# Fetches of stored weights go from SyncE's queue to GpSimd's, and the first gated phase's weights are narrowed one expert earlier

## The chip, the cores and the metric

The kernel runs on one core of a Trainium2 chip. Its time is the device time of one launch in microseconds: 1245.48 us as the median of three runs (1244.81 to 1248.36). Five engines work side by side, each with a queue of its own that it works off in the order in which it is written: TensorE (PE; its weight loads PEld), VectorE (DVE), ScalarE (ACT), GpSimd (POOL) and SyncE (SP), which here only begins DMA transfers. ScalarE and GpSimd can begin transfers too. All transfers share 16 DMA engines.

## What is computed

Three layers follow one another. Attention over 4 x 12 heads of 448 positions gives 1792 tokens of 768 values. A router sends each token to one of 8 experts; an expert is `relu(x @ w1[e]) @ w2[e]` with 1024 hidden values, times the router's probability. A gated layer ends it:

```python
x = attn_out.transpose(0, 2, 1, 3).reshape(1792, 768)
for e in range(8):
    h = np.maximum(x[mask_e] @ w1[e], 0.0)
    out[mask_e] = gate_w[mask_e, None] * (h @ w2[e])
gate = 1.0 / (1.0 + np.exp(-(out @ w_gate)))     # 768 x 1536, stored as float64
val = out @ w_val                                # 768 x 1536, stored as float64
return (gate * val @ w_out)                      # 1536 x 768, stored as float64
```

w_gate, w_val and w_out come as float64, in DRAM as pairs of 32-bit integers. The kernel itself puts each of them together as float32, which the text calls narrowing.

## The kernel before

**The stages.** Attention and the routing fill the first 378 us. The experts follow one by one (378 to 735), sorted by the number of their tokens, so that expert e works on a window of fixed size: 320, 288, 264, 248, 240, 236, 224 and 224 tokens. Then come twelve phases of the gated layer (735 to 1061; gate and value by turns, 128 columns of each half at a time, in seven products of block sums instead of eight), and the projection by w_out (1061 to 1226).

**One expert.** Everything stands under a manual schedule: each engine does what is written for it in the order of the code. The first layer has eight chunks f. Each is 18 matmuls (`hidden`: six blocks of the contraction, three products of high and low parts, by `product`, L987), then `relu`: ScalarE writes the high part of the hidden values (hhl, L1036) and VectorE the low part (L1037). The second layer has six chunks o of 24 matmuls. Each begins with two or three transposes of the next expert's window (`window_turn`, L1025; the parts xhl at L981 and L982) and ends with a copy xo on ScalarE (L1095) and a store of it, begun by ScalarE (L1096), into the array of all tokens, x2. The second layer needs all eight chunks of the first.

**The expert weights.** An expert has seven pieces, four of w1 (768 KB) and three of w2 (1 MB). SyncE loads them into three buffers "raw" (`piece_load`, L820). Behind every chunk `advance` splits half of the piece that is two ahead: ScalarE the high part (whl, L831), VectorE the low part (L835). Every second chunk it begins the load of the piece three ahead.

**What is woven in.** In experts 2 to 6, behind each of the 14 chunks, `out_narrow` takes a step: either it begins the fetch of a 128 x 384 block of w_out into one of two buffers raw64 (`out_fetch`, L1253, on SyncE), or it narrows one: four VectorE operations (L1222, L1225, L1231, L1234), an addition on GpSimd (L1237) and a store of the block to DRAM, begun by GpSimd (L1269). There are 24 blocks. `early_sums` has GpSimd form parts of the gated layer's input sums in experts 5 and 6 (L1307) and store them into x2 (L1310). In expert 7 `glu_weights` does for four blocks of w_gate, the first phase's weights B11, B12, B22 and B21, what was done for w_out (fetched on SyncE, L1348; kept on the chip), forms their sums T3, T2, T1 and T4 (L1374) and splits them (`w_split`). `glu_ahead` does three blocks of the second phase in expert 7's second layer. Narrowed blocks and early sums take turns in six buffers v. `window_load(e + 1)` (L1014 and L1016, on SyncE) fetches the next expert's tokens at the start of an expert.

**The first gated phase.** `glu` holds a table of jobs by slot (slot i stands behind the i-th of the phase's 14 groups of matmuls, counted from 0; -1 ahead of the phase): casts and differences of input blocks (`both`, `parts`, L1274 and L1277), sums of blocks (`sums`, L1307; `fourth`, L1474). Evictions of the products are L1541 and L1546.

Of the kernel before, what the change touches and what calls it, by code (L numbers as in the profile page):

```python
# [21 lines left out]
def tile_attention_moe_glu(  # L22
# [966 lines left out]
    def experts(pools):  # L989
# [55 lines left out]
        for e in range(E):  # L1045
            n = WIN[e]
            hh = ho.tile([128, 2, nfc, CAP], F32R, tag="hhl", name="hhl")[:, :, :, 0:n]
            if 0 < e < E - 1:
                window_load(e + 1)
# [11 lines left out]
            if e == 0:  # L1061
                window_load(1)
            for f in range(nfc):
                if f < ahead:
                    ps = pss4[f]
                else:
                    ps = gemm_ps()[:, :n]
                    for c in range(NC):
                        hidden(e, f, ps, c)
# [178 lines left out]
    def out_fetch(pools):  # L1248
        if out_at[0] < len(outs):
# [3 lines left out]
            nc.sync.dma_start(out=out_raw[-1][2], in_=wo64[f * 128 : (f + 1) * 128, h * ND : (h + 1) * ND])  # L1253

    def out_narrow(pools):
# [5 lines left out]
        if step < 2 or (out_at[2] and step * len(outs) // 68 == (step - 1) * len(outs) // 68):  # L1261
            out_fetch(pools) if len(out_raw) < 2 else None
        elif out_raw:
# [5 lines left out]
            nc.gpsimd.dma_start(out=wod[f][:, h * ND : (h + 1) * ND], in_=v)  # L1269

# [69 lines left out]
    fetched = {}  # L1340

    def fetch(pools, i):
        if i < len(fetches):
# [4 lines left out]
            nc.sync.dma_start(out=t, in_=w64[k % 2][:, r * HC : (r + 1) * HC, m * 128 : (m + 1) * 128])  # L1348
# [48 lines left out]

    def glu_weights(pools, f, xw):

        if f == 0:  # L1400
            ws.extend([xw[:, i].rearrange("p (a c t) -> p a c t", a=2, c=HC)[:, a] for a in range(2)] for i in range(3))
            for i in range(2):
                fetch(pools, i)
        elif f < 5:
            for step in range(2):
                v_narrow(pools, 0, V_FIRST[f - 1], step)
            if f == 2:
                w_split(pools, 0, 1)
            elif f == 3:
                v_sum(pools, 0, "T3")  # L1410
                v_sum(pools, 0, "T2")
        elif f == 5:
            w_split(pools, 0, 7)
        elif f == 6:
            w_split(pools, 0, 6)
            v_sum(pools, 0, "T1")
        elif f == 7:
            v_sum(pools, 0, "T4")
# [21 lines left out]
    def glu(pools):  # L1440
        pools["wq"].release()
# [47 lines left out]
        for slot, f, *a in (  # L1489
            (-1, both, 1, "A11"), (-1, both, 0, "S1"), (-1, sums, "S1", s1, nc.gpsimd), (-1, sums, "S2", s2, nc.gpsimd),  # L1490
            (1, both, 0, "A12"), (1, w_split, pools, 0, 5), (2, w_split, pools, 0, 2), (2, fourth),
            (3, both, 1, "A12"), (3, parts, 0, "S4", s4), (4, parts, 1, "S1", s1), (5, both, 1, "A22"),
# [270 lines left out]
```

## Time and profile before

| | |
|---|---|
| median of three runs | 1245.48 us |
| the profiled execution, its span | 1246.61 us, 1244.9 us |
| TensorE busy | 1151.9 us, 93% |
| VectorE, ScalarE, GpSimd busy | 844.6, 620.4, 532.7 us |

The profile is of one execution. In the rows below, a row of the table of stretches has the window in us, its length, the busy time of TensorE, of its weight loads, of VectorE, ScalarE and GpSimd (each with its count of instructions), the granted clock of TensorE as a share of full speed, the mean busy share of the DMA engines and GB/s. A timeline row has the start, the duration, the engine, the line, the operation, what it writes and reads, and in brackets how long the engine stood idle before it and what ended that. A row of waits says which line waited for what: us in total, times, longest. In the chain of waits each piece follows from the one above it, to the end of the program.

### The profile page before, as it was taken

What the parts mean: (1) busy time and instruction counts of PE and PEld (TensorE: products, weight loads), DVE (VectorE), ACT (ScalarE), POOL (GpSimd) and SP (SyncE); (2) the same over time, 40 slices, a digit from 0 to 9 for tenths busy, and PEclk for the clock granted to TensorE, in tenths of its full rate; (3) what the DMA queues carried; (4) which work ended last, traced back from release to release, by engine and by line L of the source; (5) the groups of instructions that cost most, each with busy time, mean ns of one, the idle gap of its engine ahead of it and who ended that gap; (6) DMA issues with size and microseconds to landing.
All of it is one profiled execution on the core that took longest, in us unless ns stands there. A gap on an engine that the chain in (4) does not pass through costs nothing.

```text
span 1244.9 us, 20296 instructions
## 1 busy us (share of the span) xinstructions
PE 1151.9 (93%) x7312; PEld 1061.2 (85%) x7313; DVE 844.6 (68%) x1424; ACT 620.4 (50%) x1363; POOL 532.7 (43%) x654
## 2 busy tenths in 40 slices
PE   4999999999968999988988887999999999999997
PEld 3778888887957999987888886999999999999997
DVE  7999898897874556678677879768776774422110
ACT  5788998998963444444434445333332324321110
POOL 5656779777430001212334253747566464011110
PEclk9999999999988999989989977999999999999999
DMA  5315613121027567777879620323223234532220
GB/s 131 92 31 161 198 46 89 48 56 33 1 80 237 161 200 243 249 248 241 262 237 304 208 90 13 104 73 130 81 96 111 76 110 150 189 127 77 89 76 38
DMA packets 125323, 161.50 MB, mean 130 GB/s; under 512 B 6495, under 2 KB 111327, under 8 KB 125219
## 3 DMA queue, kind: packets, MB, share of 16 engines
q1 hardware_dynamic: 113331, 135.86, 35.5%
q0 software_dynamic: 4704, 17.80, 4.0%
q10 hardware_dynamic: 7184, 6.50, 1.6%
q8 instruction: 59, 0.97, 0.3%
q14 instruction: 45, 0.37, 0.1%
HBM read 117.19 MB, written 34.60 MB: 122 GB/s over the span
## 4 chain that ended last, share of the span: by engine, by line
PE 50%; DVE 7%; DMA 7%; issue 2%; ACT 2%; ACTq 0%; POOL 0%; SPq 0%; POOLq 0%; DVEq 0%
PE psg L1519 24%; PE pso L987 13%; PE psg L987 12%; DMA raw<-in_moe_w_dram 5%; DVE whl L835 2%; DMA x<-xo 1%; ACT whl L831 1%; DVE v L1225 1%; PE psw L1025 1%; DMA raw<-in_moe_w_gate_dram 1%; DVE sx L1277 1%; DVE e L1234 1%; DVE x L1277 1%; PE psw L850 1%; DVE hhl L1037 1%
## 5 line engine op out<-in xcount | busy, mean ns | idle before, releaser
L1237 POOL TENSOR_TENSOR v<-v,e 128x384 f32<-128x384 f32 x72 | 74.6, 1036 | 329.3 <-DVE e L1234 318.9
L835 DVE TENSOR_TENSOR whl<-raw,whl 128x768 fp32r<-128x768 f32 (+1 forms) x112 | 137.8, 1231 | 88.3 <-ACT whl L831 85.6
L987 PE MATMUL psg<-hhl,whl 128*128 128x224 f32 (+6 forms) x1152 | 167.1, 304 | 20.9 <-DVE hhl L1037 13.1
L987 PEld LDWEIGHTS psg<-hhl,whl 128*128 128x128 f32 x1152 | 156.2, 207 | 24.3 <-DVE hhl L1037 12.0
L987 PE MATMUL psg<-xhl,whl 128*128 128x224 f32 (+6 forms) x1152 | 145.6, 285 | 8.1 <-DVE whl L835 4.8
L987 PEld LDWEIGHTS psg<-xhl,whl 128*128 128x128 f32 x1152 | 140.2, 189 | 11.9 <-DVE whl L835 6.4
L831 ACT CAST whl<-raw 128x768 fp32r<-128x768 f32 (+1 forms) x112 | 103.2, 923 | 84.2 <-DMA raw<-in_moe_w_dram 51.7
L333 ACT ACTIVATE pn<-pss,nm 112x448 f32<-112x448 f32 x184 | 119.9, 652 | 26.1 <-DVE nm L322 24.4
L322 DVE TENSOR_REDUCE nm<-pss 112x1 f32<-112x448 f32 x192 | 118.3, 616 | 11.3 <-PE pss L315 10.9
L987 PE MATMUL pso<-sx,x 128*128 128x384 f32 x720 | 125.0, 334 | 0.0
L987 PEld LDWEIGHTS pso<-sx,x 128*128 128x128 f32 x720 | 124.8, 188 | 0.0
L370 DVE TENSOR_TENSOR pl<-pst,ph 112x448 fp32r<-112x448 f32 x180 | 110.5, 614 | 18.3 <-ACT ph L357 16.9
L1519 PE MATMUL psg<-sx,xw 128*128 128x448 f32 x420 | 112.0, 375 | 2.9 <-ACT sx L1274 2.9
L350 PEld LDWEIGHTS pst<-ident,pn 112*112 112x112 f32 x768 | 88.6, 135 | 26.7 <-DVE pl L370 6.8
L350 PE MATMUL pst<-ident,pn 112*112 112x112 f32 x768 | 107.0, 262 | 4.6 <-DVE pl L370 4.3
L357 ACT CAST ph<-pst 112x448 fp32r<-112x448 f32 x180 | 97.5, 542 | 9.8 <-PE pst L350 7.0
L384 PE MATMUL psv<-ph,vt 112*128 112x448 f32 x204 | 92.1, 461 | 0.0
L315 PE MATMUL pss<-kh,qt 128*112 128x448 f32 x192 | 79.5, 414 | 12.1 <-ACT pn L333 11.0
L1519 PEld LDWEIGHTS psg<-sx,xw 128*128 128x128 f32 x420 | 81.1, 193 | 11.1 <-ACT sx L1274 3.9
L714 POOL DMA_INDIRECT out_dram<-sg,idx x14 | 17.4, 1242 | 160.0 <-DVE sg L1652 98.1
L1519 PE MATMUL psg<-sx,x 128*128 128x448 f32 x297 | 75.8, 366 | 0.9 <-DVE sx L1277 0.9
L315 PE MATMUL pss<-kl,qt 128*112 128x448 f32 x192 | 72.1, 376 | 0.0
(275 smaller groups left out, 2394.2 us busy)
## 6 DMA issues: line engine op xcount, KB each, us to landing
raw<-in_moe_w_dram SPq DMA_DIRECT2D x32, 768.0 KB, 7.1
raw<-in_moe_w_dram SPq DMA_DIRECT2D x24, 1024.0 KB, 7.7
hd<-sg SPq DMA_DIRECT2D x48, 224.0 KB, 1.9
raw<-in_moe_w_out_dram SPq DMA_DIRECT2D x24, 384.0 KB, 5.0
raw<-in_moe_w_gate_dram SPq DMA_DIRECT2D x24, 384.0 KB, 3.3
raw<-in_moe_w_val_dram SPq DMA_DIRECT2D x24, 384.0 KB, 3.4
xs<-zero SPq DMA_DIRECT2D x8, 960.0 KB, 8.1
x<-hd SPq DMA_DIRECT2D x5, 1536.0 KB, 7.6
```

The lines of the kernel that those rows point to most:

```text
L315: nc.tensor.matmul(ps[:P, :S], lhsT=qt[:, r * P : (r + 1) * P], rhs=kk, start=(i == 0), stop=(i == 1))
L322: nc.vector.tensor_reduce(out=nm, in_=sc[n, r][:P, :S], axis=AX.X, op=ALU.max, negate=True)
L333: nc.scalar.activation(out=pn[n][:, r], in_=sc.pop((n, r))[:P, :S], func=AF.Exp, bias=sc.pop((n, r, "m")), scale=scale(0, 0, n, 1)[:, r] i ...
L350: nc.tensor.transpose(ps[:P, r * P : (r + 1) * P], p[:, r, c * P : (c + 1) * P], ident[:P, :P])
L357: nc.scalar.copy(out=ph, in_=pt[n, c][0][:P, :S])
L370: nc.vector.tensor_tensor(out=pl, in0=ps[:P, :S], in1=ph.bitcast(F32), op=ALU.subtract)
L384: nc.tensor.matmul(ps[:, :S], lhsT=lhs, rhs=p, start=(c == 0 and i == 0), stop=(c == R - 1 and i == len(parts) - 1),)
L831: nc.scalar.copy(out=splits[p][:, 0, cs], in_=raws[p][:, cs])
L835: nc.vector.tensor_tensor(out=w[:, 1, cs], in0=raws[p][:, cs], in1=w.bitcast(F32)[:, 0, cs], op=ALU.subtract)
L987: nc.tensor.matmul(ps, lhsT=lhs[:, a], rhs=rhs[:, b], start=first and i == 0, stop=last and i == 2)
L1237: nc.gpsimd.tensor_tensor(out=v, in0=v, in1=e, op=ALU.add)
L1519: nc.tensor.matmul(ps, lhsT=w[a][:, c], rhs=x[b][:, c], start=(n == 0 and j in (1, 2, 7)), stop=(n == 3 * HC - 1), skip_group_check=j not ...
```

## The change

The fetches of w_out and, until the gated layer starts, of w_gate and w_val are begun by GpSimd, right behind the addition and the store of a narrowed block. The steps at which blocks are narrowed are spread by another formula (57 steps for the 24 blocks), which gives 4, 6, 6, 6 and 2 of them in experts 2 to 6. The four w_gate blocks of the first phase are narrowed at steps 61, 63, 65 and 67, which is in expert 6 (its chunks f5, f7, o1 and o3), and T3 and T2 are formed at o4 and o5; expert 7 keeps T1, T4 and the splits, at earlier chunks. The window load of the next expert stands at an expert's fourth chunk. In the first gated phase four jobs stand in later slots, so that evictions come ahead of casts.

```diff
--- before.py
+++ after.py
@@ -1045,8 +1045,6 @@
         for e in range(E):
             n = WIN[e]
             hh = ho.tile([128, 2, nfc, CAP], F32R, tag="hhl", name="hhl")[:, :, :, 0:n]
-            if 0 < e < E - 1:
-                window_load(e + 1)
             roff = nc.scalar.value_load(table_i[0:1, 2, e : e + 1], min_val=0, max_val=NT if e else 0)
             ahead = 2 if e == 0 else 0
             pss4 = [gemm_ps()[:, :n] for f in range(ahead)]
@@ -1058,9 +1056,9 @@
                 if c:
                     for f in range(ahead):
                         hidden(e, f, pss4[f], c - 1)
-            if e == 0:
-                window_load(1)
             for f in range(nfc):
+                if f == 3 and e + 1 < E:
+                    window_load(e + 1)
                 if f < ahead:
                     ps = pss4[f]
                 else:
@@ -1250,7 +1248,9 @@
             f, h = outs[out_at[0]]
             out_at[0] += 1
             out_raw.append((f, h, raw_tile(pools)))
-            nc.sync.dma_start(out=out_raw[-1][2], in_=wo64[f * 128 : (f + 1) * 128, h * ND : (h + 1) * ND])
+            nc.gpsimd.dma_start(out=out_raw[-1][2], in_=wo64[f * 128 : (f + 1) * 128, h * ND : (h + 1) * ND])
+
+    OUT_STEPS = 57
 
     def out_narrow(pools):
 
@@ -1258,15 +1258,22 @@
         out_at[1] += 1
         if step == 0:
             st_open(pools)
-        if step < 2 or (out_at[2] and step * len(outs) // 68 == (step - 1) * len(outs) // 68):
-            out_fetch(pools) if len(out_raw) < 2 else None
-        elif out_raw:
+            for _ in range(2):
+                out_fetch(pools)
+        n = len(outs)
+        if step > 2 and (step - 2) * n // OUT_STEPS > (step - 3) * n // OUT_STEPS and out_raw:
             f, h, raw = out_raw.pop(0)
             v = vs[out_at[2] % len(vs)]
             out_at[2] += 1
             narrow_a(raw, v)
             narrow_b(raw, v, es[0])
             nc.gpsimd.dma_start(out=wod[f][:, h * ND : (h + 1) * ND], in_=v)
+            if out_at[0] < n:
+                out_fetch(pools)
+            else:
+                fetch(pools, len(fetched))
+        elif step in V_STEPS:
+            glu_first(pools, V_STEPS.index(step))
 
 
 
@@ -1338,6 +1345,8 @@
     V_OF = {1: "B11", 2: "B21", 6: "T2", 7: "T3", 5: "B12", 4: "B21", 3: "B22"}
     fetches = [(k, n) for k in range(PHASES) for n in (V_NAMES if k else V_FIRST)]
     fetched = {}
+    glu_queue = [nc.gpsimd]
+    V_STEPS = (61, 63, 65, 67, 68, 69)
 
     def fetch(pools, i):
         if i < len(fetches):
@@ -1345,7 +1354,7 @@
             r, c = int(n[1]) - 1, int(n[2]) - 1
             m = k // 2 + c * HM
             t = fetched[i] = raw_tile(pools)
-            nc.sync.dma_start(out=t, in_=w64[k % 2][:, r * HC : (r + 1) * HC, m * 128 : (m + 1) * 128])
+            glu_queue[0].dma_start(out=t, in_=w64[k % 2][:, r * HC : (r + 1) * HC, m * 128 : (m + 1) * 128])
 
     V_SLOT = {"B11": 4, "B21": 5, "B12": 0, "B22": 3, "T3": 1, "T2": 2}
     V_SLOT0 = {"B11": 0, "B12": 1, "B22": 2, "B21": 3, "T3": 4, "T2": 5, "T4": 0}
@@ -1395,26 +1404,25 @@
         jobs += [(split[i], w_split, k, j) for i, j in enumerate(ORDER)]
         return jobs
 
+    def glu_first(pools, i):
+
+        if i < 4:
+            for step in range(2):
+                v_narrow(pools, 0, V_FIRST[i], step)
+        else:
+            v_sum(pools, 0, ("T3", "T2")[i - 4])
+
     def glu_weights(pools, f, xw):
 
         if f == 0:
             ws.extend([xw[:, i].rearrange("p (a c t) -> p a c t", a=2, c=HC)[:, a] for a in range(2)] for i in range(3))
-            for i in range(2):
-                fetch(pools, i)
-        elif f < 5:
-            for step in range(2):
-                v_narrow(pools, 0, V_FIRST[f - 1], step)
-            if f == 2:
-                w_split(pools, 0, 1)
-            elif f == 3:
-                v_sum(pools, 0, "T3")
-                v_sum(pools, 0, "T2")
-        elif f == 5:
+            w_split(pools, 0, 1)
+        elif f == 2:
             w_split(pools, 0, 7)
-        elif f == 6:
+        elif f == 4:
             w_split(pools, 0, 6)
             v_sum(pools, 0, "T1")
-        elif f == 7:
+        elif f == 6:
             v_sum(pools, 0, "T4")
 
     def glu_open(pools, xhl):
@@ -1438,6 +1446,7 @@
                 v_narrow(pools, 1, V_NAMES[o - 1], step)
 
     def glu(pools):
+        glu_queue[0] = nc.sync
         pools["wq"].release()
         pools["wr"].release()
         sx_pool = tc.alloc_tile_pool(name="sx", bufs=1, side="right", reuse_waits="tile")
@@ -1487,9 +1496,9 @@
             jobs.setdefault(slot, []).append((f, a))
 
         for slot, f, *a in (
-            (-1, both, 1, "A11"), (-1, both, 0, "S1"), (-1, sums, "S1", s1, nc.gpsimd), (-1, sums, "S2", s2, nc.gpsimd),
-            (1, both, 0, "A12"), (1, w_split, pools, 0, 5), (2, w_split, pools, 0, 2), (2, fourth),
-            (3, both, 1, "A12"), (3, parts, 0, "S4", s4), (4, parts, 1, "S1", s1), (5, both, 1, "A22"),
+            (-1, both, 1, "A11"), (-1, sums, "S1", s1, nc.gpsimd), (1, both, 0, "S1"), (1, w_split, pools, 0, 5),
+            (2, both, 0, "A12"), (2, w_split, pools, 0, 2), (2, sums, "S2", s2, nc.gpsimd), (3, both, 1, "A12"),
+            (3, fourth), (4, parts, 0, "S4", s4), (4, parts, 1, "S1", s1), (5, both, 1, "A22"),
             (5, parts, 1, "S2", s2), (6, w_split, pools, 0, 3), (6, sums, "S3", s1, nc.vector), (7, parts, 1, "S3", s1),
             (7, sums, "S4", s2, nc.gpsimd), (9, parts, 1, "S4", s2),
         ):
```

SyncE's queue (in the names, raw is an expert weight buffer, raw_N a buffer of int64 rows, xw a window). Before, from the second w1 piece of expert 3 (loaded in expert 2's second layer) on, to the window that is fetched at the start of expert 3:

```order
L820 ISA
L820 DMA raw<-in_moe_w_dram 128x6x256
L1253 DMA raw_7365<-in_moe_w_out_dram 128x768
L820 ISA
L820 DMA raw<-in_moe_w_dram 128x6x256
L1253 DMA raw_7481<-in_moe_w_out_dram 128x768
L1008 TENSOR_LOAD table_i
L1008 ISA x2
L1008 TENSOR_LOAD table_i
L1008 ISA x2
L1014 ISA
L1014 DMA xw<-xs 128x768
```

And now, from the third w1 piece of expert 3 to the same window:

```order
L820 ISA
L820 DMA raw<-in_moe_w_dram 128x6x256
L820 ISA
L820 DMA raw<-in_moe_w_dram 128x6x256
L820 ISA
L820 DMA raw<-in_moe_w_dram 128x8x256
L1008 TENSOR_LOAD table_i
L1008 ISA x2
L1008 TENSOR_LOAD table_i
L1008 ISA x2
L1014 ISA
L1014 DMA xw<-xs 128x768
```

The fetches of w_out are gone from between the loads, and the window load stands behind the fourth w1 piece and the first w2 piece, which came after it.

GpSimd's queue among the narrowings, from the addition of one block on, before (v_N and e_N are the two parts that the addition puts together):

```order
L1237 TENSOR_TENSOR v_7038<-v_7038,e_7039 128x384
L1269 DMA wod<-v_7038 128x384
L1237 TENSOR_TENSOR v_7033<-v_7033,e_7039 128x384
L1269 DMA wod<-v_7033 128x384
L1237 TENSOR_TENSOR v_7034<-v_7034,e_7039 128x384
```

And now, from the store of the fourth block on, in expert 2 and 3:

```order
L1270 DMA wod<-v_7015 128x384
L1251 DMA raw_7438<-in_moe_w_out_dram 128x768
L1235 TENSOR_TENSOR v_7016<-v_7016,e_7018 128x384
L1270 DMA wod<-v_7016 128x384
L1251 DMA raw_7517<-in_moe_w_out_dram 128x768
L1235 TENSOR_TENSOR v_7017<-v_7017,e_7018 128x384
```

Pairs of addition and store have become triples of addition, store and the fetch of a later block.

VectorE's queue in expert 7's first layer, before:

```order
L1037 SCALAR_TENSOR_TENSOR hhl<-psg,hhl 128x224
L835 TENSOR_TENSOR whl<-raw,whl 128x768
L1222 TENSOR_SCALAR v_7035<-raw_9552 128x384
L1225 SCALAR_TENSOR_TENSOR v_7035<-raw_9552,v_7035 128x384
L1231 TENSOR_SCALAR e_7039<-v_7035 128x384
L1234 SCALAR_TENSOR_TENSOR e_7039<-raw_9552,e_7039 128x384
L1374 TENSOR_TENSOR v_7037<-v_7035,v_7034 128x384
L1374 TENSOR_TENSOR v_7038<-v_7037,v_7033 128x384
L1037 SCALAR_TENSOR_TENSOR hhl<-psg,hhl 128x224
L835 TENSOR_TENSOR whl<-raw,whl 128x1024
```

And now:

```order
L1037 SCALAR_TENSOR_TENSOR hhl<-psg,hhl 128x224
L835 TENSOR_TENSOR whl<-raw,whl 128x768
L1037 SCALAR_TENSOR_TENSOR hhl<-psg,hhl 128x224
L835 TENSOR_TENSOR whl<-raw,whl 128x768
L1037 SCALAR_TENSOR_TENSOR hhl<-psg,hhl 128x224
L835 TENSOR_TENSOR whl<-raw,whl 128x768
L1037 SCALAR_TENSOR_TENSOR hhl<-psg,hhl 128x224
L835 TENSOR_TENSOR whl<-raw,whl 128x768
L1037 SCALAR_TENSOR_TENSOR hhl<-psg,hhl 128x224
L835 TENSOR_TENSOR whl<-raw,whl 128x1024
```

The narrowings and the sums between the low parts hhl and the weight splits whl are gone from here; they stand in expert 6 now.

## Rows read from the trace of the kernel before

**Rows 1.** Table of stretches: experts 1 to 7, then the first gated phase; columns explained above

```profile
431.00:478.00 47.00, 47.00 (x350) 45.66 (x348) 25.20 (x46) 21.00 (x37) 0.00 (x0) 1.00 0.58 186
478.00:516.26 38.26, 36.51 (x303) 36.30 (x302) 29.44 (x46) 19.09 (x34) 6.34 (x8) 1.00 0.85 276
516.26:559.61 43.35, 38.78 (x302) 37.69 (x301) 29.53 (x49) 18.67 (x34) 7.78 (x10) 0.92 0.77 249
559.61:603.83 44.22, 38.01 (x302) 36.83 (x301) 33.49 (x51) 20.76 (x36) 9.00 (x10) 0.92 0.74 241
603.83:648.89 45.06, 38.53 (x302) 37.22 (x301) 31.63 (x49) 18.23 (x34) 18.07 (x22) 0.92 0.83 263
648.89:690.21 41.32, 36.81 (x303) 35.60 (x301) 31.99 (x50) 18.32 (x34) 18.06 (x22) 0.96 0.85 264
690.21:735.40 45.19, 38.27 (x291) 37.03 (x289) 36.58 (x54) 18.40 (x31) 12.94 (x11) 0.85 0.55 173
735.40:780.90 45.50, 35.84 (x137) 29.14 (x136) 38.96 (x45) 25.34 (x43) 25.11 (x18) 0.81 0.07 21
```

**Rows 2.** Timeline of TensorE, expert 3's second layer: start, us, instruction

```profile
547.84 3.00 PE L987 MATMUL psg<-hhl,whl 128*128 128x248 f32 x24
550.67 0.37 PE L1025 MATMUL psw<-ident,xw 128*128 128x128 f32 x2
```

**Rows 3.** Waits of SyncE's queue, 478 to 768: us in total, times, longest

```profile
SPq L1253 <- DVE hhl L1037: 75.1, 12, 10.9
SPq L1253 <- DVE xhl L982: 72.0, 9, 9.5
SPq L1348 <- DVE v L1222: 15.9, 1, 15.9
```

**Rows 4.** Waits of the other engines, 478 to 690: us in total, times, longest

```profile
ACT whl L831 <- DMA raw<-in_moe_w_dram: 38.9, 13, 5.4
...
PE psg L987 <- DVE hhl L1037: 9.1, 5, 2.9
...
ACT whl L831 <- DMA x<-v: 6.2, 1, 6.2
```

**Rows 5.** Chain of waits, in order of time: start, us, what

```profile
629.64 5.42 DMA x<-v
...
707.50 7.06 DMA raw<-in_moe_w_dram
...
767.07 294.36 PE psg L1519 x1430
```

**Rows 6.** Timeline of GpSimd in expert 5: start, us, instruction

```profile
612.85 1.01 POOL L1237 TENSOR_TENSOR v<-v,e 128x384 f32<-128x384 f32 x1 [3.03 <-DVE e L1234]
614.15 0.57 POOL L1269 DMA_DIRECT2D wod<-v  x1 [0.30 <-POOL v L1237]
614.75 0.93 POOL L1307 TENSOR_TENSOR v<-x 128x336 f32<-128x336 f32 x1
...
616.77 0.91 POOL L1307 TENSOR_TENSOR v<-x 128x336 f32<-128x336 f32 x1
```

**Rows 7.** DMA issues, 478 to 690: count, KB each, median us to landing

```profile
raw<-in_moe_w_dram SPq DMA_DIRECT2D x15, 1024.0 KB, 11.2
...
raw<-in_moe_w_out_dram SPq DMA_DIRECT2D x22, 384.0 KB, 3.2
wod<-v POOLq DMA_DIRECT2D x24, 192.0 KB, 5.5
x<-v POOLq DMA_DIRECT2D x12, 168.0 KB, 6.8
```

**Rows 8.** Timeline of VectorE in expert 3, one narrowing and what follows

```profile
539.23 0.35 DVE L1222 TENSOR_SCALAR v<-raw 128x384 int32<-128x384 int32 x1
...
541.16 0.41 DVE L1037 SCALAR_TENSOR_TENSOR hhl<-psg,hhl 128x248 fp32r<-128x248 f32 x1
```

**Rows 9.** Timeline of VectorE, first gated phase: its first instruction

```profile
740.36 2.28 DVE L1277 TENSOR_TENSOR sx<-x,sx 128x1344 fp32r<-128x1344 f32 x1 [5.14 <-ACT sx L1274]
```

## Prediction

> **What bounds the kernel now.** I went from the whole to one wait. The table of stretches came first: one row for each expert from the second on and one for the first gated phase [rows 1]. The reader is to see that in expert 1 TensorE is busy 47.00 of 47.00 us at a granted clock of 1.00, and that from expert 3 on every stretch has both idle time and a lower clock. I call a stretch's loss its idle time plus its busy time times what the clock lacks: expert 2 1.75; expert 3 4.57 + 38.78 x 0.08 = 7.7; expert 4 6.21 + 3.04 = 9.3; expert 5 6.53 + 3.08 = 9.6; expert 6 4.51 + 1.47 = 6.0; expert 7 6.92 + 5.74 = 12.7. That is 47.0 us for the experts, and 9.66 + 6.81 = 16.5 for the gated phase. A check on expert 3: in its undisturbed second layer 24 matmuls took 2.83 us (547.84 to 550.67) and two transposes 0.14 [rows 2]; 288 matmuls and six such pairs are 34.8, so the loss is 43.35 - 34.8 = 8.5, near the 7.7.
>
> Then the waits of SyncE's queue [rows 3]: 75.1 + 72.0 = 147 us in which the head of that queue was a fetch of a w_out row block (L1253) that stood until VectorE had narrowed the block two before it, and 15.9 us at once for a gate fetch (L1348). Behind each stand the loads of the expert weights, in order. The waits of the other engines say who pays [rows 4]: ScalarE waited 38.9 us in 13 pieces for expert weights to land, and TensorE 9.1 us in five pieces for VectorE's low part of the hidden values, up to 2.9 at once; that is the change of layer, where the eighth chunk's low part stands in VectorE's queue behind delayed weight splits. The chain of waits has the same [rows 5]: near its end a load of 7.06 us in expert 7 that began at 707.50, and from 767.07 on 294.36 us of TensorE alone. So what is won before 767 is won in the end, and no gated phase after the first can win.
>
> **The change part by part.**
>
> *The fetches leave SyncE's queue.* SyncE then holds only expert weights and windows, and each weight load starts when its own buffer is free. No byte is added: the DMA engines were busy 0.77 of 43.35 us in expert 3, 33.4 us, and 0.83 of 45.06 in expert 5, 37.4 [rows 1]. These are floors under those stretches if traffic cannot be shifted to a neighbour.
>
> *GpSimd issues them behind its addition and store.* A store cost GpSimd 0.57 us of its queue, an addition with its gap 1.30 (612.85 to 614.15) [rows 6]; I price a fetch like the store, 0.57; it may cost nothing, or the 1.09 that lie between the end of an early sum and the next one (616.77 - 614.75 - 0.93), where a DMA of more rows is begun. It waits for nothing new: its buffer is the one that VectorE has just read, for which the addition ahead of it has waited already. GpSimd was busy 18.07 of 45.06 at the most among the experts up to the sixth [rows 1], so 0.57 for each of some 22 fetches is hidden, except in expert 5 (below). The landing of such a fetch is not in the trace. From below: the same 384 KB begun by SyncE landed in 3.2 us; from above 11.2, the 1 MB pieces on the same DMA engines; I take 5.5, the nearest row by issuer (GpSimd's stores) [rows 7]. Room: a buffer is refilled for the narrowing after next, mostly five steps on. A narrowing holds VectorE 1.93 us (539.23 to 541.16) [rows 8]; then come addition 1.30, store 0.57, fetch 0.57: 4.4 in all. A step in expert 3 at the forecast pace is 36.9 / 14 = 2.64, so five steps leave 13.2 - 4.4 = 8.8 and four leave 6.1; the worst, four first-layer steps of 18 matmuls (18 x 2.83 / 24 = 2.12 each), leaves 4.1, and there 5.5 comes 1.4 late, into VectorE's free time. At 5.5 the term is nothing.
>
> *More even narrowings.* The numbers per expert are 4, 6, 6, 6 in experts 2 to 5; expert 6 takes the last two of w_out and four of the gated weights. VectorE's work is about that of before (it is 29.53 of 43.35 in expert 3, 33.49 of 44.22 in expert 4) plus 1.93 where one is added.
>
> Stage by stage: **Expert 2**: 1.75 lost, mostly one wait at the layer change: -1 (bounds -1.75 and 0). **Expert 3**: weight loads are in time; three narrowings stand ahead of the eighth chunk's low part, VectorE would be 29.53 / 36.9 = 80% busy; I take -6.5 of 8.5, and 36.9 us is above the DMA floor of 33.4 (bounds -7.7 and -2). **Expert 4**: VectorE reaches 33.49 + 1.93 = 35.4 us; one stall of the 2.9 kind stays at the layer change and with it part of the lower clock: half the loss, -4.5 (bounds -8 and 0). **Expert 5**: ScalarE waited 6.2 us for GpSimd's last early sum to land (x<-v) before it could store a result [rows 4]. GpSimd now has six sums of 2.02 and two triples of addition, store and fetch ahead of that landing: 12.1 + 2 x (1.30 + 0.57 + 0.57) = 17.0; begun two first-layer steps (4.2) into the expert and with 6.8 for the landing [rows 7] it comes at 28, 3.2 earlier than now (629.64 + 5.42 - 603.83 = 31.2) [rows 5]. VectorE's splits and a narrowing at the first output chunk are late next. The DMA floor of 37.4 allows more, the chain does not: -1.5 (bounds -3.3 and 0). **Expert 6**: the narrowing of B11 at chunk 5 overwrites a v buffer that an early sum has left through a DMA, and needs its own fetch; four narrowings are as many as went: -1 (bounds -4 and +2). **Expert 7** sheds four narrowings and two sums (the narrowings alone are 4 x 1.93 = 7.7 of VectorE's 36.58), and the two gate fetches that held SyncE and with it the load at 707.50. With nothing late but the first chunk after the layer change: -11 of 12.7 (bounds -12.7 and -6; -6 is the idle time with one stall of 0.9 left).
>
> *Window loads at chunk 3.* They move behind two expert-weight loads in SyncE's queue and are needed by the transposes of the second layer, five first-layer steps (10.6 us) later. In expert 1 no wait of TensorE exists that could show them late. Nothing.
>
> *First gated phase.* VectorE's chain begins at 740.36, after ScalarE's cast, which waited for the last store of expert 7 [rows 9], and runs to 767. The jobs in front are put in another order, the additions on GpSimd are fewer beside it; what GpSimd does later it does beside later casts. Nothing, bounds -3 and +3.
>
> Sum: -1 - 6.5 - 4.5 - 1.5 - 1 - 11 = -25.5. The profiled execution took 1246.61, 1.7 more than its span of 1244.9; 1246.6 - 25.5 = 1221.1. The median of the runs is 1.1 below the profiled one, so the forecast is **1220**. All bounds together give -40 (1205) and -3 (1242).
>
> On the one queue against the other a row stands against a rule. The waits at L1253 are waits in order, 147 us, and not the cost of beginning a transfer. The Trainium skill, "Trainium Kernel Development and Optimization", section Key Constraints, says that DMAs from the SP, ACT and POOL queues run on the same 16 engines and interleave, so that more issuers only save issue time. By that alone the sum would be nothing and the time 1245; the 15.9 us in which expert weights stood behind a fetch that was not ready speak against it.
>
> **The rivals.**
>
> *A second resource is the bound (0.20).* The stalls are renamed, since VectorE at up to 35 us and the DMA engines at 33 to 37 us per expert already fill most of a stretch. For it: ScalarE's waits for weights are spread over all experts [rows 4], and in expert 5 the engines were busy 0.83. Then experts 2 to 6 gain nothing or little and only expert 7 gains, some 10: 1246.6 - 10 - 1.1 = 1235. Against it: 0.77 and 0.74 in experts 3 and 4 are with late starts.
>
> *Nearly all stalls go (0.13).* If the stretches come out at full clock and experts 4 to 6 lose only the bounds on the good side: 1205. Against it: the early sums of experts 5 and 6 stay.
>
> *The fetches land late (0.07): slower.* VectorE's queue is in order, so a narrowing that waits for its raw block holds the weight split and the low part behind it, and TensorE waits. At a landing of 11.2 us the 18 fetches with five steps' room are late by 2.4 and the four with four steps by 5.1: 43 + 20 = 63 us; 34.4 of waits are in experts 2 to 6 already and expert 7 still gives 11: 63 - 34.4 - 11 = +18, 1263. It decides from the landing at which 18 (L - 8.8) + 4 (L - 6.1) reaches 45.4, which is 10.4 us. Against it: GpSimd's own transfers landed in 5.5 and 6.8 [rows 7]. The Trainium skill, "SBUF — State Buffer", section SBUF: two separate sides, warns that a DMA begun by GpSimd has its descriptors written by GpSimd, which VectorE can lock out, and advises SP or ACT instead; by that rule this rival would hold. The trace speaks for less: stores issued beside a busy VectorE took 0.57 us of GpSimd [rows 6].
>
> *The change does not take what it aims at (0.02):* expert weights would be late by their own buffers, and the time 1245.
>
> **How the numbers follow.** Forecast 0.58 (1212 to 1230 by itself), the rivals 0.20, 0.13, 0.07, 0.02. The range 1205 to 1238 leaves out the late fetches, no change and the outer parts of two rivals, some 0.17. Within 0.3%, 3.7 us, is what a measurement of this kernel can't tell from no change: no change 0.02 and a tail of the second-resource rival 0.02 make 0.04; slower 0.07; faster 0.89.
>
> **What would show it.** Right: no fetch of w_out in SyncE's queue and hardly a wait of ScalarE for expert weights in experts 3, 4 and 7; a landing of 4 to 7 us for GpSimd's fetches; expert 3 near 37, expert 4 near 40, expert 5 near 43.5, expert 6 near 40, expert 7 near 34, the gated phase within 3 of 43 to 46; a granted clock near 1 in experts 3 and 7. Wrong: VectorE waiting for raw blocks of w_out, ScalarE still 30 us or more behind expert weights, or TensorE's idle time unchanged in experts 3 and 4. The prediction is wrong if expert 7 gains under 6, or if the first gated phase moves by more than 3.

## The result and the profile after

The changed kernel took 1228.93 us as the median of four runs (1227.57 to 1230.18); its ratio to the kernel before is 0.9857 (95% interval 0.9835 to 0.9879). The forecast was 1220 in a range of 1205 to 1238. By the profiled executions the gain is 16.4 us (spans 1244.9 and 1228.5), where the sum had 25.5: experts 2 to 7 gave 20.8, the first gated phase took 6.3 back, and the end of the program gave 2.2 that no term of the sum held (the other stages differ by 0.3).

The stages below run from a stage's first matmul to the next one's, in one profiled execution of each kernel, in us. Expert 0 and 1 are the same in all. The kernels below the second row are those of the experiments, which are told further down. Each ratio is to runs of the kernel before that were taken beside it; their medians were 1246.9 for the changed kernel and 1244.6 to 1245.3 for the others.

| kernel | e2 | e3 | e4 | e5 | e6 | e7 | gated phase | median | ratio to before, interval |
|---|---|---|---|---|---|---|---|---|---|
| before | 38.2 | 43.4 | 44.2 | 45.1 | 41.3 | 45.2 | 43.7 | 1246.9 | |
| changed | 36.3 | 36.6 | 42.2 | 44.1 | 45.2 | 32.3 | 50.0 | 1228.9 | 0.9857 (0.9835-0.9879) |
| fetch_on_sp | 38.8 | 43.1 | 43.5 | 47.5 | 48.1 | 35.8 | 45.2 | 1247.6 | 1.0025 (1.0009-1.0040) |
| before_fetch_gpsimd | 39.4 | 36.5 | 41.0 | 42.3 | 39.5 | 43.5 | 48.8 | 1237.2 | 0.9939 (0.9917-0.9961) |
| gate_narrow_in_e7 | 36.2 | 38.2 | 41.2 | 44.4 | 42.0 | 43.4 | 50.0 | 1237.7 | 0.9943 (0.9922-0.9965) |
| window_at_start | 36.4 | 37.4 | 42.4 | 44.8 | 44.9 | 32.3 | 49.5 | 1231.3 | 0.9885 (0.9861-0.9910) |
| p0_old_order | 36.4 | 36.5 | 39.6 | 43.7 | 46.3 | 32.3 | 48.9 | 1227.3 | 0.9878 (0.9852-0.9903) |
| sp_from_e7_second | 36.3 | 36.7 | 42.5 | 44.2 | 45.5 | 32.3 | 45.2 | 1225.4 | 0.9834 (0.9797-0.9871) |
| e6_no_early_sums | 36.3 | 36.6 | 41.6 | 44.4 | 41.0 | 32.3 | 49.1 | 1224.7 (one run) | |
| fourth_block_in_e7 | 36.4 | 36.6 | 41.6 | 44.2 | 43.4 | 32.3 | 49.5 | 1225.1 | 0.9841 (0.9809-0.9873) |
| both_mends | 36.3 | 36.6 | 41.2 | 44.2 | 43.8 | 32.3 | 45.5 | 1221.5 | 0.9811 (0.9792-0.9829) |
| two_blocks_in_e7 | 36.2 | 36.6 | 41.2 | 45.1 | 40.7 | 35.8 | 45.8 | 1224.2 | 0.9843 (0.9824-0.9862) |
| both_mends_old_jobs | 36.2 | 36.6 | 41.2 | 44.4 | 42.1 | 32.3 | 44.3 | 1218.7 | 0.9795 (0.9772-0.9819) |

Stages that are written alike differ from one execution to another: expert 4 by 39.6 to 42.5 and expert 6 by 42.1 to 43.8 and 45.2 to 46.3, so one execution settles nothing under 2 to 3 us there.

The table of stretches of the changed kernel, to be laid beside [rows 1] (the same columns):

```profile
478.21:514.55 36.34, 36.34 (x303) 36.20 (x302) 27.42 (x42) 19.11 (x34) 6.34 (x9) 1.00 0.77 237
514.55:551.12 36.57, 34.91 (x302) 34.42 (x301) 33.12 (x53) 18.88 (x34) 12.65 (x18) 1.00 0.93 309
551.12:593.27 42.15, 37.60 (x303) 36.61 (x301) 35.20 (x55) 20.99 (x36) 15.13 (x18) 0.92 0.84 268
593.27:637.33 44.06, 37.54 (x303) 36.71 (x302) 37.30 (x53) 18.64 (x34) 22.93 (x30) 0.92 0.89 280
637.33:682.48 45.15, 39.15 (x302) 37.96 (x301) 40.92 (x57) 18.50 (x34) 23.30 (x28) 0.89 0.87 272
682.48:714.76 32.28, 32.28 (x291) 32.24 (x289) 25.65 (x35) 18.40 (x31) 10.26 (x10) 1.00 0.50 157
714.76:764.50 49.74, 35.50 (x127) 28.83 (x126) 43.01 (x48) 24.60 (x42) 20.12 (x19) 0.76 0.11 32
```

In experts 2 and 7 TensorE is busy without a gap at a granted clock of 1.00. Expert 3 has 1.66 us of idle time left instead of 4.57. In experts 4 to 6 VectorE is busy 35.20 of 42.15, 37.30 of 44.06 and 40.92 of 45.15, more than before, and the granted clock is 0.92, 0.92 and 0.89. The gated phase is longer, at 0.76.

The waits of the engines, 478 to 682 us, to be laid beside [rows 4], then those of SyncE's queue beside [rows 3], and the DMA issues beside [rows 7]:

```profile
PE psg L987 <- DVE hhl L1037: 11.8, 6, 4.0
ACT whl L831 <- DMA raw<-in_moe_w_dram: 10.3, 4, 2.9
```

```profile
SPq L820 <- DVE xhl L982: 62.5, 10, 7.9
...
SPq L820 <- DMA raw<-in_moe_w_dram: 0.7, 1, 0.7
```

```profile
raw<-in_moe_w_dram SPq DMA_DIRECT2D x15, 1024.0 KB, 9.1
raw<-in_moe_w_dram SPq DMA_DIRECT2D x20, 768.0 KB, 6.0
raw<-in_moe_w_out_dram POOLq DMA_DIRECT2D x22, 384.0 KB, 6.0
```

ScalarE waits 10.3 us for expert weights instead of 38.9. SyncE's queue waits for nothing but buffers of expert weights. A w_out fetch lands in 6.0 us (5.5 was taken). But TensorE still waits 11.8 us for the low part of the hidden values, where it was 9.1. From 752.74 on the chain is TensorE alone, as it was from 767.07 on [rows 5], for as long:

```profile
752.74 294.47 PE psg L1528 x1430
```

That start is 14.3 us earlier; the other 2 us of the span's 16.4 lie behind the last matmul. The program ends 8.8 us after it in the two kernels whose w_out fetches SyncE begins (before and fetch_on_sp), and 6.0 to 6.7 us after it in the eleven others. What takes longer there was not tried.

### The profile page after: what moved, and what is told of

Its sections match the earlier page's. It is cut to its first block, busy times and chain, and to the rows that moved or that the text cites. A ratio compares the mean times of both kernels' runs of the same rounds, so it can differ in the third digit from the quotient of the medians.

```text
span 1228.5 us, 20258 instructions
## 1 busy us (share of the span) xinstructions
PE 1145.3 (93%) x7312; PEld 1056.8 (86%) x7313; DVE 857.8 (70%) x1424; ACT 622.0 (51%) x1363; POOL 548.8 (45%) x687
## 4 chain that ended last, share of the span: by engine, by line
PE 69%; DVE 11%; ACT 7%; DMA 5%; issue 4%; POOL 3%; ACTq 0%; POOLq 0%; SPq 0%; DVEq 0%
PE psg L1528 24%; PE psg L987 16%; PE pso L987 13%; PE pss L315 4%; PE psv L384 4%; PE pst L350 3%; ACT pn L333 2%; PE pso L400 2%; DMA raw<-in_moe_w_dram 2%; DVE nm L322 1%; DVE whl L835 1%; ACT ph L357 1%; DVE sx L1284 1%; PE psk L277 1%; DVE st L195 1%
## 5 line engine op out<-in xcount | busy, mean ns | idle before, releaser
L835 DVE TENSOR_TENSOR whl<-raw,whl 128x768 fp32r<-128x768 f32 (+1 forms) x112 | 143.6, 1284 | 57.4 <-ACT whl L831 55.1
L987 PE MATMUL psg<-hhl,whl 128*128 128x224 f32 (+6 forms) x1152 | 159.5, 296 | 16.2 <-DVE hhl L1037 11.8
L987 PEld LDWEIGHTS psg<-hhl,whl 128*128 128x128 f32 x1152 | 149.3, 198 | 19.2 <-DVE hhl L1037 13.0
```

Of the source, the lines that this page charges most:

```text
L835: nc.vector.tensor_tensor(out=w[:, 1, cs], in0=raws[p][:, cs], in1=w.bitcast(F32)[:, 0, cs], op=ALU.subtract)
L987: nc.tensor.matmul(ps, lhsT=lhs[:, a], rhs=rhs[:, b], start=first and i == 0, stop=last and i == 2)
```

## The experiments

Each experiment names two theories, A and B, with the result that each would give.

**The queue alone, from both sides.** The changed kernel with its fetches begun by SyncE:

```diff
-            nc.gpsimd.dma_start(out=out_raw[-1][2], in_=wo64[...])
+            nc.sync.dma_start(out=out_raw[-1][2], in_=wo64[...])
-    glu_queue = [nc.gpsimd]
+    glu_queue = [nc.sync]
```

> The changed kernel with the same fetches at the same places of the code, but begun by SyncE: w_out blocks, and the gated weights until the gated layer starts. Theory A, the order on SyncE's queue was the cost (my prediction's first step): expert weights are again behind fetches that wait for VectorE, ScalarE's waits for expert weights go from 10 us back to 30 or more, experts 3 and 4 together lose 6 to 9 us and expert 7 little, since its narrowings are gone; the time is 1236 to 1240. Theory B, where the narrowings stand decides and the queue does not: since a fetch now stands right behind the narrowing, SyncE's wait for it is short; time within 3 us of 1229.

It took 1247.58 us: all of the gain is lost and more than theory A said. Its waits in 478 to 698, and SyncE's in 478 to 735:

```profile
ACT whl L831 <- DMA raw<-in_moe_w_dram: 62.6, 18, 7.4
```

```profile
SPq L1251 <- DVE xhl L982: 70.3, 11, 9.7
SPq L1251 <- DVE hhl L1037: 61.5, 9, 12.7
```

ScalarE is back at 62.6 us behind expert weights, since the head of SyncE's queue stood 132 us for w_out, though here each fetch is written right behind its narrowing. Expert 7, from which theory A expected little, grows by 3.5 (32.3 to 35.8). And the kernel before with nothing changed but the queue (four lines, as above, in the kernel before):

> The kernel before with nothing changed but the queue: its fetches of w_out, and of the gated weights up to the gated layer, are begun by GpSimd at the same steps; narrowings, windows and jobs stand as before. Theory A, the queue is the whole gain (all fetches on SyncE gave 1247.6 with the changed kernel's steps): experts 3 and 4 fall by 3 to 6 us each, expert 7 by 3 to 5 (its weight loads are free, its narrowings stay), the time is 1230 to 1236. Theory B, GpSimd's queue only helps with the fetch right behind the addition, since at other steps it waits in GpSimd's order as it waited in SyncE's: the time is 1243 to 1247.

1237.24 us, a little above theory A's 1236. Experts 2 to 7 take 15.1 us less (3 to 6 alone 14.6), and the gated phase 5.1 more. So the queue gives the gain of experts 3 to 6; what the changed kernel adds is expert 7 (43.5 to 32.3) and 3.1 in expert 2, and it pays for them in experts 4 to 6 (122.8 to 131.4).

**The narrowings of expert 6 back in expert 7.**

```diff
-    V_STEPS = (61, 63, 65, 67, 68, 69)
+    V_STEPS = ()
     def glu_weights(pools, f, xw):
+        elif f < 5:
+            for step in range(2):
+                v_narrow(pools, 0, V_FIRST[f - 1], step)
...
```

> The changed kernel with the four w_gate blocks of the first phase, their sums and their splits back in expert 7 as before; fetches stay with GpSimd. In the changed kernel expert 6 took 45.15 us (41.32 before) and expert 7 32.28 (45.19 before). Theory A, VectorE's time is what is short in either place: expert 6 falls to about 39, expert 7 rises to about 39 (VectorE 25.65 + 4 x 1.93 + 4 x 0.75 for the weight split stretched beside each addition + two sums of 0.55 = 37.5 us busy), so the time is about the same, 1228 to 1231. Theory B, it was the place alone that cost in expert 7 (order on SyncE's queue): expert 7 stays at 33 to 34 without the SyncE queue's waits and expert 6 falls to 39, so the time falls to 1224 or less.

1237.73 us, 8.8 above the changed kernel. Its expert 6 and expert 7, in the columns of [rows 1]:

```profile
636.09:678.04 41.95, 37.96 (x302) 37.04 (x301) 31.55 (x41) 18.60 (x34) 17.10 (x21) 0.92 0.84 268
678.04:721.41 43.37, 36.66 (x290) 35.60 (x289) 35.13 (x51) 18.29 (x31) 16.23 (x16) 0.88 0.47 140
```

Both theories missed. Expert 7 goes to 43.37, though SyncE's queue is free; VectorE is busy 35.13 (37.5 was expected), and the lower clock, 0.88, costs on top. VectorE waited for no block in expert 7's first layer. So most of expert 7's long time before was the narrowings themselves, set between its low parts and weight splits. The order on SyncE's queue is the smaller part: it is worth 1.7 with the narrowings there (45.2 before, 43.5 in before_fetch_gpsimd) and 3.5 without them (35.8 in fetch_on_sp, 32.3 in the changed kernel).

**The gated phase.** First the order of its jobs, put back as it was:

```diff
-            (-1, both, 1, "A11"), (-1, sums, "S1", s1, nc.gpsimd), (1, both, 0, "S1"), (1, w_split, pools, 0, 5),
...
+            (-1, both, 1, "A11"), (-1, both, 0, "S1"), (-1, sums, "S1", s1, nc.gpsimd), (-1, sums, "S2", s2, nc.gpsimd),
...
```

> The changed kernel with the first gated phase's jobs in the order of before, all else as changed. In the changed kernel that phase took 49.96 us (714.76 to 764.72) against 43.71 before; one VectorE difference (sx, 128x1344) lasted 9.98 us while GpSimd ran eight operations back to back, where before none lasted over 2.5. Theory A, the new order of jobs puts GpSimd's sums against VectorE's first difference at a bad moment: the phase falls back to about 44.5 us and the time to about 1223.5. Theory B, the phase is longer because expert 7 now ends with fewer waits and its last store lands later against the casts (3.85 us instead of 2.94), whatever the order: the phase stays at 49 to 50 us and the time at 1229.

The phase stays at 48.94, so theory A falls; the time is 1227.28. Theory B's result came, but its reason is only a part of it, as VectorE and GpSimd of the changed kernel show at the end of expert 7 and the start of the phase (714.76; timelines: start, us, instruction, idle before):

```profile
708.19 0.35 DVE L1220 TENSOR_SCALAR v<-raw 128x384 int32<-128x384 int32 x1
...
709.57 0.56 DVE L1232 SCALAR_TENSOR_TENSOR e<-raw,e 128x384 f32<-128x384 uint32 x1
...
716.71 0.36 DVE L1220 TENSOR_SCALAR v<-raw 128x384 int32<-128x384 int32 x1 [3.96 <-DMA raw<-in_moe_w_val_dram]
...
720.63 9.98 DVE L1284 TENSOR_TENSOR sx<-x,sx 128x1344 fp32r<-128x1344 f32 x1 [1.92 <-ACT sx L1281]
730.53 1.54 DVE L1284 TENSOR_TENSOR x<-x,sx 128x1344 fp32r<-128x1344 f32 x1
```

```profile
710.26 1.01 POOL L1235 TENSOR_TENSOR v<-v,e 128x384 f32<-128x384 f32 x1 [3.38 <-issue]
712.58 0.79 POOL L1357 DMA_DIRECT2D raw<-in_moe_w_val_dram  x1 [1.31 <-DVE e L1229]
713.39 1.02 POOL L1235 TENSOR_TENSOR v<-v,e 128x384 f32<-128x384 f32 x1
...
718.87 1.00 POOL L1235 TENSOR_TENSOR v<-v,e 128x384 f32<-128x384 f32 x1 [3.75 <-DVE e L1232]
719.82 0.78 POOL L1357 DMA_DIRECT2D raw<-in_moe_w_gate_dram  x1
720.62 3.35 POOL L1314 TENSOR_TENSOR sg<-x 128x448 f32<-128x448 f32 x3
723.93 1.99 POOL L1284 TENSOR_TENSOR x<-v,x 128x384 fp32r<-128x384 f32 x2
725.89 3.30 POOL L1314 TENSOR_TENSOR acc<-sg,x 128x448 f32<-128x448 f32 x3
```

The third narrowing needs the buffer of the first, which VectorE had read by 710.13 (709.57 + 0.56). Its fetch stands behind the addition, which ended at 711.27, waited 1.31 more (for VectorE, by the profile), began at 712.58 and landed by 716.7; VectorE waited 3.96. Its addition then begins at 718.87, and the sums for the phase at 720.62, 5.86 after the phase; before, the last addition began at 735.37 and the sums at 736.34, 0.94 after it. At 720.6 they meet VectorE's first difference, which lasts 9.98 us while eight GpSimd operations run at their 1.0 to 1.1 each; before it lasted 2.28 [rows 9]. The test is one line, with which SyncE begins these fetches again:

```diff
     def glu_ahead(pools, o):
         if o == 0:
+            glu_queue[0] = nc.sync
```

> The changed kernel with the second phase's weights fetched by SyncE again from expert 7's second layer on (one line); everything before that with GpSimd. In the changed kernel and with the phase's old job order the first gated phase took 49.96 and 48.94 us; with all fetches on SyncE 45.17. In the changed kernel the third narrowing of that layer waited 3.96 us for its block, which GpSimd had begun behind its addition, and GpSimd's sums for the phase began 5.9 us after the phase (720.62 against 714.76) where before they began 0.9 after it. Theory A, this late fetch makes the sums late, and they then stand against VectorE's first difference: the phase falls to 44 to 45.5 us, the time to 1223.5 to 1225. Theory B, the phase is long for another reason, such as stores of expert 7 that land later at full speed: the phase stays at 48 or more and the time at 1229.

The phase takes 45.19 us, the time 1225.44, about as theory A had it, though its reason covers only some 3 of the 4.8 us, as the chain below shows. The phase does not hang on one execution: in the seven kernels in which GpSimd begins the fetches of expert 7's second layer it takes 48.8 to 50.0, in the five after the change in which SyncE does 44.3 to 45.8 (43.7 before it). The same rows there:

```profile
714.23 0.48 DVE L1220 TENSOR_SCALAR v<-raw 128x384 int32<-128x384 int32 x1 [0.88 <-DMA raw<-in_moe_w_val_dram]
...
719.47 1.69 DVE L1284 TENSOR_TENSOR sx<-x,sx 128x1344 fp32r<-128x1344 f32 x1 [3.10 <-ACT sx L1281]
721.11 2.48 DVE L1284 TENSOR_TENSOR x<-x,sx 128x1344 fp32r<-128x1344 f32 x1
```

```profile
716.51 1.02 POOL L1235 TENSOR_TENSOR v<-v,e 128x384 f32<-128x384 f32 x1 [2.02 <-DVE e L1232]
717.48 4.69 POOL L1314 TENSOR_TENSOR sg<-x 128x448 f32<-128x448 f32 x3
722.13 4.63 POOL L1284 TENSOR_TENSOR x<-v,x 128x384 fp32r<-128x384 f32 x2
```

VectorE waits 0.88 for the block instead of 3.96, the sums begin 2.05 after the phase (715.43), and the first difference takes 1.69 while GpSimd's three sums take 4.69 instead of 3.35: the two share here.

The chain of waits shows a second part. In the changed kernel, and then in sp_from_e7_second, it goes from the last store of expert 7 (start, us in flight) over ScalarE's cast to VectorE's first difference:

```profile
715.33 3.85 DMA x<-xo
...
720.63 9.98 DVE sx L1284
```

```profile
716.00 2.01 DMA x<-xo
...
719.47 1.69 DVE sx L1284
```

With SyncE's fetches the store lands 1.84 us sooner, and the way from the first difference to ScalarE's cast of the finished sums takes 15.06 us (719.47 to 734.53) instead of 18.01 (720.63 to 738.64), 2.95 less: together the 4.8. So the later stores of theory B are the smaller part, and come with the same fetches; in the five kernels the store takes 1.99 to 2.06, in the seven 2.54 to 4.17. Nor is it the hold of 9.98 alone: in fourth_block_in_e7 and window_at_start the first difference takes 5.52 and 5.70, and the phase 49.5 all the same. Why the store lands later was not tried.

**Expert 6.** Without its early sums:

```diff
+            if e < 6:
                 x_sum(pools, 0, cols, name, t, nc.gpsimd)
                 x_place(pools, 0, cols, name, t, nc.gpsimd)
```

> The changed kernel without the six early sums of expert 6 and their stores (a part of the gated layer's input sums is left out). Expert 6 took 45.15 us with 40.92 of VectorE busy. Theory A, VectorE is the bound there because each GpSimd operation beside it stretches its weight splits (1.7 us and up to 2.37 where 0.96 stands alone): without six sums VectorE is busy some 36 us and the expert takes 38 to 41. Theory B, the number of narrowings and their fetches decide, the sums are hidden: 44 to 46.

Expert 6 takes 41.01 us in this one execution, VectorE 34.84. Below are its weight splits of 768 columns and the first step of its narrowings, and above them those of the changed kernel (groups by shape: count, busy us, mean ns, idle before):

```profile
L835 DVE TENSOR_TENSOR whl<-raw,whl 128x768 fp32r<-128x768 f32 x9 | 12.9, 1438 | 2.5 <-ACT whl L831 2.5
...
L1220 DVE TENSOR_SCALAR v<-raw 128x384 int32<-128x384 int32 x7 | 5.2, 740 | 0.0
```

```profile
L835 DVE TENSOR_TENSOR whl<-raw,whl 128x768 fp32r<-128x768 f32 x9 | 11.5, 1282 | 3.1 <-ACT whl L831 3.1
...
L1220 DVE TENSOR_SCALAR v<-raw 128x384 int32<-128x384 int32 x7 | 2.5, 352 | 1.1 <-DMA raw<-in_moe_w_out_dram 1.1
```

Nine splits take 1282 ns each instead of 1438, and the seven first steps of a narrowing, which theory A did not name, 352 instead of 740, which is the largest part. VectorE is relieved as theory A said, and the time is at the upper end of its range. How an addition and a sum stretch what is beside them, in expert 6 of the changed kernel (VectorE, then GpSimd; the expectation's 2.37 is a split of 1024 columns, which takes 1.21 alone):

```profile
644.34 0.94 DVE L835 TENSOR_TENSOR whl<-raw,whl 128x768 fp32r<-128x768 f32 x1
...
648.14 1.71 DVE L835 TENSOR_TENSOR whl<-raw,whl 128x768 fp32r<-128x768 f32 x1
...
650.07 2.34 DVE L835 TENSOR_TENSOR whl<-raw,whl 128x768 fp32r<-128x768 f32 x1
652.34 1.48 DVE L1220 TENSOR_SCALAR v<-raw 128x384 int32<-128x384 int32 x1
```

```profile
648.02 1.01 POOL L1235 TENSOR_TENSOR v<-v,e 128x384 f32<-128x384 f32 x1 [0.89 <-DVE e L1232]
...
649.89 0.77 POOL L1357 DMA_DIRECT2D raw<-in_moe_w_gate_dram  x1
650.68 0.91 POOL L1314 TENSOR_TENSOR v<-x 128x336 f32<-128x336 f32 x1
651.89 0.78 POOL L1317 DMA_DIRECT2D x<-v  x1 [0.29 <-POOL v L1314]
652.68 0.91 POOL L1314 TENSOR_TENSOR v<-x 128x336 f32<-128x336 f32 x1
```

A split that begins alone takes 0.94, beside the addition 1.71, beside one sum and the two transfers that GpSimd begins around it 2.34, and the first step of the narrowing behind it, beside the next sum, 1.48 instead of 0.35. Then one narrowing fewer in expert 6, which keeps two of w_out and three of w_gate, the latter two steps later:

```diff
-    V_STEPS = (61, 63, 65, 67, 68, 69)
+    V_STEPS = (63, 65, 67, -1, 68, 69)
     def glu_weights(pools, f, xw):
+        elif f == 1:
+            glu_first(pools, 3)
```

> The changed kernel with the four w_gate narrowings two steps later: B11, B12, B22 at expert 6's chunks f7, o1 and o3, and B21 in expert 7 at its second chunk. Expert 6 then has four narrowings in its 14 steps after the two of w_out instead of six in all five, expert 7 four instead of three; VectorE was busy 25.65 of 32.28 in expert 7. Theory A, expert 6's first layer is bound by VectorE and GpSimd together: it loses one narrowing and one addition there, 1.93 + 0.75 = 2.7, so expert 6 falls to 42 to 43 and expert 7 stays within 0.5: 1226 to 1227. Theory B, expert 6 waits for weights and landings instead: 45 again, and time 1229 or a little more.

Expert 6 takes 43.40 us, expert 7 32.28 as before the move; 1225.08. The direction is theory A's, with 1.8 instead of 2.7. One execution would not settle that, but the three kernels with this placement have 42.1 to 43.8 in expert 6, the four with the changed kernel's (window_at_start among them) 44.9 to 46.3. VectorE's time is not all that sets this stage: in gate_narrow_in_e7 expert 6 has no w_gate narrowing and VectorE is busy 31.55, yet it takes 41.95.

**The window load.**

```diff
+            if 0 < e < E - 1:
+                window_load(e + 1)
...
-                if f == 3 and e + 1 < E:
-                    window_load(e + 1)
```

> The changed kernel with the window load of the next expert back at an expert's start (for expert 0 ahead of its chunks). Theory A, no expert waits for a window and the DMA engines have room: within 2 us of 1229, experts 3 to 6 within 1 us each. Theory B, the earlier window load delays the expert weights behind it at the start of an expert, when the DMA engines are fullest (0.93 busy in expert 3): experts 3 to 6 each 1 us longer, 1232 to 1234.

1231.32 us, by stages 0.8 more in expert 3 and at most 0.7 in another. The intervals overlap: where the load stands is worth nothing, or some 2 us.

**The mends together.**

> The changed kernel with both mends: the second phase's fetches by SyncE from expert 7's second layer on, and B21 narrowed in expert 7. By itself the first took the first gated phase from 49.96 to 45.19 us, the second took expert 6 from 45.15 to 43.40. Theory A, they are in different stages and add: -4.8 - 1.7, 1222 by the median of 1228.9. Theory B, what expert 6 gives up comes back because expert 7 then ends nearer its limit and the phase starts against later transfers: 1224 to 1226.

1221.45 us. They add. Then one more block and both sums go back to expert 7 (the edit is to the kernel with both mends):

```diff
-    V_STEPS = (63, 65, 67, -1, 68, 69)
+    V_STEPS = (65, 67)
     def glu_weights(pools, f, xw):
         if f == 0:
+            glu_first(pools, 2)
...
+        elif f == 3:
+            glu_first(pools, 3)
```

> As the kernel with both mends, but with two w_gate blocks (B22, B21) and both sums in expert 7's first layer and only B11 and B12 in expert 6, at its chunks o1 and o3. Theory A, expert 6's first layer is then relieved of every gated narrowing and falls to 40 to 41.5; expert 7's VectorE, 25.65 busy, takes two narrowings, two stretched splits and two sums, 25.65 + 3.86 + 1.5 = 31 of 32.28, and expert 7 grows by 0.5 to 2: 1220 to 1222. Theory B, expert 7's first layer is where VectorE has no room, as with all four narrowings back there (43.37): expert 7 grows by 4 or more, 1223 to 1226.

1224.24 us: expert 6 falls to 40.7, but expert 7 grows by 3.6 to 35.84, with VectorE busy in 90% of it:

```profile
636.00:676.71 40.71, 35.22 (x303) 33.93 (x301) 36.30 (x49) 19.41 (x36) 19.64 (x24) 1.00 0.89 282
676.71:712.55 35.84, 32.93 (x291) 32.38 (x289) 32.27 (x45) 18.22 (x31) 11.28 (x12) 1.00 0.54 173
```

It is between the theories, nearer to B. Last, both mends with the phase's old jobs (the edit of the order above):

> As the kernel with both mends, with the first gated phase's jobs in the order of before. With the late fetch in place that order took 48.94 us instead of 49.96. Theory A, once the sums begin in time, the new order (evictions ahead of casts, the S2 sums later) is worth nothing or little: within 1.5 us of the kernel with both mends. Theory B, the new order of jobs is worth 2 us or more when nothing is late: 2 us or more slower.

1218.71 us, the least of all, 0.9795 of before against 0.9811; the intervals overlap. That is 2.7 less, further than theory A's 1.5 and on the other side from theory B. The phase takes 44.33 instead of 45.54, and with the late fetches the old order was 1.0 shorter as well. So the new order of jobs is worth nothing, and may cost 1; the two profiled executions also differ by 1.7 in expert 6, which is written alike in both.

## Why the prediction was right, and where it was not

*The fetches leave SyncE's queue*: right. Both kernels that change the queue alone show it: the changed kernel loses 18.7 us without it, and the kernel before wins 14.6 in experts 3 to 6 with it, where the sum had 13.5 for queue and narrowings together. The changed kernel wins only 6.0 there; it narrows 24 blocks in these experts instead of 19. The Trainium skill, "Trainium Kernel Development and Optimization", section Key Constraints, has it that several issuers only save issue time. The runs differ from that where a queue's head waits: the same transfers on the same engines, 18.7 us apart.

*GpSimd's fetch costs nothing*: for w_out right, with a landing of 6.0 and no narrowing late. Its failing is expert 7's second layer: the room was worked out for a fetch five steps ahead of its use, and there three narrowings stand at three steps in a row over two buffers. The room is then two steps, and the third narrowing waited 3.96 us.

*Experts 2 to 7*, forecast and measured: -1 and -1.8; -6.5 and -6.8; -4.5 and -2.1 (-4.6 in another execution of the same code); -1.5 and -1.0; -1 and +3.8; -11 and -12.9. The step that failed is expert 6's. It counted "four narrowings are as many as went" and asked only for a buffer and a fetch. The count is wrong: expert 6 had four narrowings of w_out before, two of these stay and four of w_gate come, so it has six. With the one that spills over from expert 5, its stretch holds seven instead of five. A narrowing was priced at 1.93 us of VectorE, without what GpSimd's addition adds to the split beside it (0.94 to 1.71). VectorE's time there rose by 8.9, from 31.99 to 40.92 us. Leaving the sums out takes 4.1 us off, one narrowing less 1.8. Expert 5's reason was wrong as well: ScalarE no longer waits for an early sum there, TensorE waits for VectorE at the change of layer. That looks like the second-resource rival, in experts 4 to 6 and not in 3 and 7; only in expert 6 was it tried, by taking work from VectorE.

*Expert 7*: the size was right, the reason half. With its narrowings and free queues it takes 43.4, so the narrowings were most of the cost; the order on SyncE's queue, with the load that began at 707.50 [rows 5], was 1.7 of it.

*The first gated phase*: "Nothing, bounds -3 and +3" failed; it is +6.3, more than the 3 that the prediction itself named as a sign of being wrong. It looked at the order of jobs and at the additions, not at the fetches that expert 7's second layer begins, which moved to GpSimd as well. One line gives 4.8 back.

*The total*: the time lies in the range although two terms were far off, by 4.8 us in expert 6 and 6.3 in the phase. In part that is luck: expert 7 gave 1.9 more than forecast, and the end of the program 2.2 that no term held.

*The fetches land late* (the slower rival) had the right mechanism at one place, and not at the 22 fetches it was worked out for. The Trainium skill, "SBUF — State Buffer", section SBUF: two separate sides, warns of VectorE starving GpSimd's DMAs. The runs bear it out at most in part: GpSimd's fetches of w_out took 0.54 us each to begin and landed in 6.0, SyncE's in 3.2 to 3.4, so they are slower, but in the changed kernel none was late. Whether VectorE is what slows them was not tried.

## What to carry to other kernels

A transfer whose buffer comes free late belongs on a queue on which nothing urgent stands behind it; ask of each moved transfer, at each place where it is begun, how far off its use is there. When waits for transfers go, the next bound is the engine whose work was spread by them: count its time with what a neighbour's operations add to it, not alone. A filler moved from one stage to another is worth it as long as its new stage has room for it, and a kernel can have one block too many on either side.

## What was not expected of the hardware

VectorE's difference of two operands was held 9.98 us by a series of eight GpSimd operations that ran at full speed (10.40 in the run without early sums). In fourth_block_in_e7 and window_at_start it was held 5.52 and 5.70, by four such operations, and the next four shared. In sp_from_e7_second and before the two shared from the first difference on, VectorE at 1.7 to 2.5 and GpSimd at 1.6 to 2.3 for an operation. Which began first does not tell them apart: in the changed kernel GpSimd's series began 0.01 us ahead of VectorE's operation, without the early sums 0.43 behind it (715.73 and 715.30), in sp_from_e7_second 2 us ahead. In fourth_block_in_e7 it began 0.21 ahead. What decides was not tried.
